# Attention, gated feed-forward and routed experts on one core: the first expert's first matrix in two loads behind the last stores, the late products one accumulator at a time, and a new order of the experts

## Chip, cores and metric

One core of a Trainium2 chip runs the whole program in one launch. The metric is device time in microseconds (us). Engines: PE (TensorE, matrix products), DVE (VectorE), ACT (ScalarE), POOL (GpSimd), SP (SyncE, which here only issues DMAs).

## What is computed

```python
for t in range(S):                                  # attention with a delta-rule state, 32 heads
    y[:, :, t] = einsum('bhd,bhde->bhe', q[:, :, t], state)
    state += beta * k_n (v - state k_n)
...
h = x @ w_in                                        # 3072 x 384 times 384 x 2048
g = P(h) / (Q(h) + 1e-06)                           # P cubic, Q quadratic in |h|
x2 = g @ w_out                                      # 3072 x 384
...
order = argsort(-(x2 @ w_gate).flatten())           # 3072 tokens x 8 experts
# best pairs first; a token goes to one expert, an expert takes at most 384 tokens
for e in range(8):
    out[assigned == e] = relu(x2[assigned == e] @ w1[e]) @ w2[e]
```

The order in which experts fill up depends on the data, so the kernel finds one expert after another: it looks for the first to reach 384 tokens, fixes its tokens, takes expert and tokens out, and looks again.

## The kernel before

The program has a prologue, a loop over 12 chunks of the sequence (attention, feed-forward, gate logits), a drain of the last chunk (`drain`), and the last stage (`tail`) with the choice of experts and their products. All the edits that change the order of work lie between the end of `drain` and the end of the program.

**Late products.** The rows of the last chunk, x2 = g @ w_out, are 96 products of 128x384 into two accumulators in PSUM, px0 and px1 (list `T['late']`, line 1021, 48 products for each). Seven are made in `drain`, the others in `Experts.late` (line 804, products at L761) between the steps of the first choice. ACT moves each accumulator to a tile `yo` (L808), and SP stores it in two DMAs (L809) to the scratch tensor x2d in DRAM, from which the tokens of an expert are gathered.

**The choice of one expert** (`Route.phase`) is a chain between PE and DVE. Six times: count products (L673, or L680 in the first choice), DVE masks the counts (cs, L677), PE folds them (L675), DVE flags full experts (fl, L685), PE spreads the flags (L686), DVE takes the digit (dd, y) and compares anew (ge, L617). `close` then gives the expert's number, the row numbers `ix` of its weights (L706), and the tokens it takes. `perm` turns them into a list of row numbers (pc, o at L739, pD, the list product at L751, `perm` at L757).

**One expert** (`Experts`). `load` (line 778) issues two indirect DMAs from POOL, one for each matrix, 128 rows of 3072 float32 each (L782), and splits each of the 16 pieces of 128x384 into a high part (ACT, L793) and a low part (DVE, L794). `gather` fetches 3 x 128 rows of x2d (POOL, L799). `transp` transposes them on PE (L816) and splits them (xe: ACT L819, DVE L820). `up` has 8 groups of 9 products (L828); after each, ACT takes the relu's high part (L831), and the low part comes from DVE (L833) or, where the table's `rp` is 1 and the planner prefers it, from a product on PE that subtracts the high part (L832) and a relu on ACT (L834). `down` is 3 x 24 products (L841), an eviction to `yo` by ACT (L843) and an indirect store by POOL (L846). Weights are loaded one choice ahead: that of expert k+1 stands between `up` and `down` of expert k.

**What sets the order.** Every step is added to a planner (`Sched`) with an engine, a planned duration, the data that it needs and a priority from the table `PR` (8 numbers for each kind of step, one for each expert). `Sched.run` plays it through and writes out, engine by engine, the order so found; the engines run that order strictly and wait on semaphores, so a step that waits holds up all that stands behind it on its engine. Where the plan shows PE idle before the first transposition, dummy products are put in (L1555).

Of the kernel before, what the change touches and what calls it, by code (L numbers as in the profile page):

```python
# [517 lines left out]
class Ring:  # L518
# [4 lines left out]
PR=dict(cz=[-8460.22,-3349.02,-1040.92,-4662.57,2286.09,-4542.55,-2851.07,-2830.4],  # L523
    hu=[-1158.71,2769.58,-1952.33,1420.35,20.61,-5092.86,1294.98,-2930.25],
    pm=[-827.35,-3434.29,-7199.64,-301.76,-9380.25,-789.5,-2507.28,-3094.98],
    px=[2213.47,-717.87,711.27,1083.3,-50.99,-1678.84,-176.44,-42.49],
    ev=[-2031.38,3896.44,-445.84,4974.79,-456.6,1410.8,-187.26,-280.73],
    rs=[3995.53,-838.36,3724.15,-2030.4,-5106.28,-2002.19,4963.77,-277.67],
    up=[1432.01,7925.78,415.8,19527.06,1302.29,-2496,-1028.3,393.52],
    dn=[-416.52,-263.26,2914.53,2346.47,7002.88,3039.18,1234.23,2541.59],  # L530
    sp=[-1250.53,-1034.63,-3233.17,3355.56,-2061.84,10814.9,2205.04,145.63],
    sq=[1182.66,5658.8,2518.53,1693.88,5502.59,2521.4,11976.42,-493.54],
    ga=[-91.9,220.07,-1393.31,1453.88,1738,-498.56,-1773.97,252.48],
    ld=[-763.16,-1461.53,2155.57,-1535.71,-2478.81,4661.21,334.89,-1356.37],
    sc=[1792.56,3025.86,-3657.49,-269.42,-11268.81,2802.89,972.48,366.12],
    de=[868.62,405.65,-1417.99,2091.14,378.47,2357.24,-3935.23,-63.01],
    rp=[1,0,0,0,0,0,0,0],
    sl=[9.7,-3928.78,-7440.7,1542.96,-6870.28,-1220,4305.31,-2018.78],
    lt=3989.8,
    tol=0.3)  # L540
class Route:
# [3 lines left out]
    def __init__(s,ctx,tc,c):  # L545
# [28 lines left out]
        s.rows=c.tile([128,1],F32,name="rowid"); s.iota(s.rows,[[0,1]],base=128*E,cm=1)  # L574
        s.mk,s.fold={},{}
# [116 lines left out]
    def close(s):  # L692
# [13 lines left out]
        s.V(.07,lambda: v.scalar_tensor_tensor(ix,cm,-128.0,s.rows,op0=OP.mult,op1=OP.add),[cmn],[ixn],.16-z)  # L706
# [55 lines left out]
class Experts:  # L762
# [16 lines left out]
    def load(s,n,ixn,late=[]):  # L779
# [3 lines left out]
        g.add(('POOL',1.038,ld(a,s.w1,"p g j q -> p (g j q)")),[ixd],fa,P1,post=0.7); g.add(('DMA',4.4,None),fa,fa,0,post=0.9)  # L783
        g.add(('POOL',1.038,ld(b,s.w2,"p j f -> p (j f)")),[ixd]+late,fb,P1,post=0.7); g.add(('DMA',4.4,None),fb,fb,0,post=0.9)
# [10 lines left out]
    def gather(s,n,pmn):  # L795
        g=s.g; nc=s.nc; pm,pmd=pmn; s.st.setdefault(n,{})['pm']=pmn; s.st[n]['x']=s.xe.new()
        for i in range(3):
            t,tn=s.xg.new(); s.st[n]['g',i]=t,tn
            g.add(('POOL',1.038,lambda t=t,i=i: nc.gpsimd.indirect_dma_start(out=t,out_offset=None,in_=s.x2d,in_offset=bass.IndirectOffsetOnAxis(ap=pm[:,i:i+1],axis=0))),[pmd,'x2d'],[tn],PR['ga'][n],post=0.7)  # L799
            g.add(('DMA',.55,None),[tn],[tn],0,post=1.0)  # L800
    def late(s,M,T):
# [3 lines left out]
        for bp in range(2):  # L805
# [4 lines left out]
            g.add(('ACT',.371,out),[('epy',bp)],[o_n],20)  # L810
            g.add(('DMA',2.5,None),[o_n],[o_n,'x2d'],0)
# [23 lines left out]
    def down(s,n):  # L835
        g=s.g; nc=s.nc; W2,W2n=s.st[n]['W2']; pm,pmd=s.st[n]['pm']; r,rn=s.st[n]['r']; pd=PR['dn'][n]; pe=PR['de'][n]
        for i in range(3):
# [11 lines left out]
            g.add(('POOL',1.08,out),[o_n,pmd],[('sc',o_n)],PR['sc'][n],post=0.7)  # L849
            g.add(('DMA',.55,None),[('sc',o_n)],[o_n,('sc',o_n)],0,post=1.0)  # L850
LG=1
def tail(R,X,M,T):
    g=R.g=X.g=Sched(); g.tol=PR['tol']; X.late(M,T)
# [126 lines left out]
def drain(g,M,A,R,st,xT,x2d,Lt):  # L980
# [40 lines left out]
    T['late']=[(un,i,bp,gh,wh) for un in range(u0,u0+8) for i in range(2) for bp in range(2) for gh,wh in ((0,0),(0,1),(1,0))]; px=[('px',bp) for bp in range(2)]  # L1021
# [5 lines left out]
    for n,x in enumerate(T['late'][:EL]): add(('PE',.172,go(x,n==0)),[('lg',0),('lg',1)],px if n==0 else [px[x[2]]],1e6+n)  # L1027
# [592 lines left out]
```

## Time and profile before

| | us |
|---|---|
| median of 3 runs (863.96 to 866.63) | 866.54 |
| the profiled execution: time | 867.04 |
| the profiled execution: span, first to last instruction | 865.3 |
| busy over the span: PE, DVE, ACT, POOL | 808.9, 739.5, 563.8, 416.8 |
| mean granted clock of PE, as a share of full speed | 0.979 |

Each row of a timeline has its start and duration in us, counted from the span's first instruction, then engine, line, operation, the names that it writes and reads, and in brackets how long its engine had been idle and what ended that. A row with x9 stands for nine instructions that follow each other. Rows by stretch give for each engine the busy time and the number of instructions, then the granted clock, the busy share of the DMA engines and GB/s. The last late product ends about us 610, the first product of the first expert starts at 626.61, the last product ends about 857.5, and the last stores end the span.

### The profile page before, as it was taken

What the parts mean: (1) busy time and instruction counts of PE and PEld (TensorE: products, weight loads), DVE (VectorE), ACT (ScalarE), POOL (GpSimd) and SP (SyncE); (2) the same over time, 40 slices, a digit from 0 to 9 for tenths busy, and PEclk for the clock granted to TensorE, in tenths of its full rate; (3) what the DMA queues carried; (4) which work ended last, traced back from release to release, by engine and by line L of the source; (5) the groups of instructions that cost most, each with busy time, mean ns of one, the idle gap of its engine ahead of it and who ended that gap; (6) DMA issues with size and microseconds to landing.
All of it is one profiled execution on the core that took longest, in us unless ns stands there. A gap on an engine that the chain in (4) does not pass through costs nothing. (4 is left out here: it accounts for less than half of the span.)

```text
span 865.3 us, 29590 instructions
## 1 busy us (share of the span) xinstructions
PE 808.9 (93%) x12536; PEld 581.0 (67%) x12536; DVE 739.5 (85%) x1696; ACT 563.8 (65%) x1039; POOL 416.8 (48%) x620
## 2 busy tenths in 40 slices
PE   8999789998999999999999999999899899999896
PEld 5887566776677767777777777766556556556563
DVE  8977987888889998998999999996889899889820
ACT  4236767888698787988888889881272451545520
POOL 2256820888678567865786232631221322242501
PEclk9999889999999999999999999999999999999999
DMA  9943387813532524251322201000450542355401
GB/s 362 280 137 84 103 203 211 248 62 75 116 85 81 107 83 97 82 108 31 87 75 67 42 21 39 19 2 20 146 220 29 191 184 112 109 201 229 155 11 45
DMA packets 89588, 98.62 MB, mean 114 GB/s; under 512 B 65776, under 2 KB 73584, under 8 KB 86640
## 3 DMA queue, kind: packets, MB, share of 16 engines
q1 hardware_dynamic: 83072, 59.31, 26.2%
q0 software_dynamic: 6096, 37.23, 11.7%
q8 instruction: 98, 1.61, 0.8%
q14 instruction: 34, 0.28, 0.1%
q10 hardware_dynamic: 288, 0.20, 0.1%
HBM read 74.43 MB, written 17.30 MB: 106 GB/s over the span
## 5 line engine op out<-in xcount | busy, mean ns | idle before, releaser
L936 PEld LDWEIGHTS <-wi 128*128 128x128 f16 x1728 | 168.6, 99 | 38.1 <-issue 6.3
L882 PE MATMUL px<-wo,gg 128*128 128x392 f16 (+1 forms) x1056 | 193.5, 330 | 0.0
L882 PEld LDWEIGHTS <-gg 128*128 128x128 f16 x1056 | 97.8, 98 | 61.8 <-issue 0.7
L900 POOL TENSOR_TENSOR gg<-w,gg 128x512 f16<-128x512 f32 x61 | 71.1, 1166 | 99.6 <-ACT gg L899 92.7
L936 PE MATMUL half<-xT,wi 128*128 128x256 f16 x864 | 107.1, 280 | 3.7 <-DVE wo L1320 2.5
L936 PE MATMUL ph<-xT,wi 128*128 128x256 f16 x864 | 104.2, 275 | 4.5 <-DVE w L913 2.3
L206 POOL TENSOR_TENSOR pmW<-pmW,pmT 128x31 f32<-128x31 f32 (+15 forms) x155 | 89.7, 579 | 10.8
L205 POOL TENSOR_TENSOR pmT<-pmW,pmA 128x31 f32<-128x31 f32 (+15 forms) x155 | 81.3, 525 | 10.9
L841 PEld LDWEIGHTS <-rr 128*128 128x128 f16 x576 | 52.1, 97 | 34.7 <-ACT rr L831 2.8
L846 POOL DMA_INDIRECT out_dram<-yo,perm x24 | 24.3, 1013 | 100.9 <-ACT yo L843 95.5
L831 ACT ACTIVATE rr<-eph 128x384 f16<-128x384 f32 x64 | 30.8, 488 | 59.5 <-PE eph L828 54.4
L899 ACT ACTIVATE gg<-w 128x512 f16<-128x512 f32 x88 | 55.4, 629 | 7.2 <-DVE w L913 6.7
L926 ACT ACTIVATE q<-q 128x512 f32<-128x512 f32 x88 | 54.8, 628 | 4.6 <-DVE q L925 4.5
L841 PE MATMUL px<-wo,rr 128*128 128x384 f16 x288 | 52.7, 330 | 2.4 <-ACT rr L831 2.3
L828 PE MATMUL eph<-xe,w1s 128*128 128x384 f16 x288 | 51.7, 333 | 1.5 <-ACT xe L819 1.0
L841 PE MATMUL px<-w2s,rr 128*128 128x384 f16 x288 | 52.9, 325 | 0.2 <-DVE w2s L794 0.2
L828 PE MATMUL eph<-xe,wo 128*128 128x384 f16 x288 | 51.7, 325 | 0.4 <-ACT xe L819 0.4
L799 POOL DMA_INDIRECT xg<-x2d,perm x24 | 26.4, 1100 | 46.9 <-issue 14.7
L1525 PE MATMUL px<-warm 128*128 128x256 f16 x344 | 44.6, 285 | 2.4 <-DVE warm L1505 2.4
L843 ACT ACTIVATE yo<-px 128x384 f32<-128x384 f32 x24 | 11.5, 490 | 44.9 <-PE px L841 35.7
L828 PEld LDWEIGHTS <-w1s 128*128 128x128 f16 x288 | 26.9, 99 | 19.7 <-issue 3.6
L925 DVE SCALAR_TENSOR_TENSOR q<-q,cf,ph 128x512 f32<-128x512 f32 x44 | 32.4, 737 | 8.7 <-ACT q L919 5.8
(398 smaller groups left out, 1897.6 us busy)
## 6 DMA issues: line engine op xcount, KB each, us to landing
kt<-in_k_dram SPq DMA_DIRECT2D x20, 512.0 KB, 4.5
kn<-in_k_dram SPq DMA_DIRECT2D x12, 384.0 KB, 4.7
qt<-in_q_dram SPq DMA_DIRECT2D x24, 192.0 KB, 3.8
vn<-in_v_dram SPq DMA_DIRECT2D x12, 384.0 KB, 4.4
x2d<-xr SPq DMA_DIRECT2D x44, 96.0 KB, 2.2
xT<-xs SPq DMA_DIRECT2D x22, 144.0 KB, 2.7
wsi<-in_moe_w_in_dram SPq DMA_DIRECT2D x3, 1024.0 KB, 5.4
wst<-in_moe_w_out_dram SPq DMA_DIRECT2D x8, 384.0 KB, 6.2
```

Of the source, the lines that this page charges most:

```text
L205: if half==0: eng.tensor_tensor(t,W[:,0:r,j:j+1].to_broadcast([n,r,k]),A[:,j:j+1,j+1:32].to_broadcast([n,r,k]),op=OP.mult)
L206: else: eng.tensor_tensor(W[:,0:r,j+1:32],W[:,0:r,j+1:32],t,op=OP.subtract)
L828: g.add(('PE',.169,lambda P=P,wh=wh,xh=xh,j=j,f=f,part=part: nc.tensor.matmul(P,W1[:,wh,f,j],xe[:,xh,j],start=(part,j)==(0,0),stop=(part,j ...
L831: g.add(('ACT',.42,lambda P=P,f=f: nc.scalar.activation(r[:,0,f],P,AF.Relu,scale=1.0-2.0**-11)),[Pn],[(rn,0,f)],pe)
L841: g.add(('PE',.17,lambda P=P,rh=rh,wh=wh,f=f,part=part,i=i: nc.tensor.matmul(P,r[:,rh,f,128*i:128*i+128],W2[:,wh,f],start=(f,part)==(0,0), ...
L882: te.matmul(T['px',un//8][bp][:,0:O.N],gg()[:,gh,i,128*bp:128*bp+128],M.wo[:,wh,fb,0:O.N],start=fb==0 and n==0,stop=fb==15 and n==2,skip_g ...
L899: ac.activation(T['gg',un][:,0].rearrange("p f t -> p (f t)")[:,a:b],T['w',un][:,a:b],AF.Copy)
L900: def gl(e): return lambda: e.tensor_tensor(T['gg',un][:,1].rearrange("p f t -> p (f t)")[:,a:b],T['w',un][:,a:b],T['gg',un][:,0].rearrang ...
L925: add(('DVE',.07+.6*z,lambda: ve.scalar_tensor_tensor(q(),q(),cf[:,4:5],P(),op0=OP.add,op1=OP.mult)),Q+Pn,Q,un+O.pd('mu',un))
L926: add(('ACT',.22+.37*z,lambda: ac.activation(q(),q(),AF.Abs)),Q,Q,un+O.pd('f2',un))
L936: for wh,xh in ((0,0),(0,1),(1,0)): te.matmul(T['P',un][:,i],M.wi[:,wh,part,128*fb:128*fb+128],xT()[:,xh,part],start=n==0,stop=n==8); n+=1
L1525: for _ in range(n): nc.tensor.matmul(bk[t or 'px1'][:,0:256],warm[:,0:128],warm,start=True,stop=True)
```

## The change

1. The list of late products has the accumulator as its outermost loop: all 48 products of px0, then all 48 of px1. The two evictions stand where they stood on ACT.
2. The first expert's first matrix comes in two indirect DMAs of 128 rows of 1536. POOL first copies one number from `yo1`, so it waits for the second eviction; then it issues the first half. The second half is issued behind the gathers, right ahead of the second matrix. Row numbers for half rows (`ix2`) are made by one more DVE instruction in the first `close`.
3. Planned durations of the POOL issues become 1.27 us (from 1.038 and 1.08); the planned store of x2d becomes 0.5 us and 2.3 us to landing (from 2.5).
4. The table `PR` is another one, so the order of the last stage is another one. Its `rp` now allows the product L832 for the first three experts (before: for the first).

```diff
-    rp=[1,0,0,0,0,0,0,0],
+    rp=[1,1,1,0,0,0,0,0],
...
+        s.rows2=c.tile([128,2],F32,name="rows2"); s.iota(s.rows2,[[1,2]],base=256*E,cm=2); s.ix2=c.tile([128,2],I32,name="ix2")
...
+        def fx():
+            if first: v.scalar_tensor_tensor(s.ix2,cm.to_broadcast([128,2]),-256.0,s.rows2,op0=OP.mult,op1=OP.add)
+            v.scalar_tensor_tensor(ix,cm,-128.0,s.rows,op0=OP.mult,op1=OP.add)
+        s.V(.07,fx,[cmn],[ixn],.16-z)
...
+        def l1(lo,hi): return lambda: nc.gpsimd.indirect_dma_start(out=a[:,lo:hi].rearrange("p g j q -> p (g j q)"),out_offset=None,in_=s.w1.rearrange('r (h c) -> (r h) c',h=2),in_offset=bass.IndirectOffsetOnAxis(ap=s.ix2[:,lo//4:lo//4+1],axis=0))
+        l2=ld(b,s.w2,"p j f -> p (j f)")
+        def half(): nc.gpsimd.tensor_copy(s.sp,s.yo.t[1][0:1,0:1]); l1(0,4)()
+        def both(): l1(4,8)(); l2()
...
-            g.add(('DMA',2.5,None),[o_n],[o_n,'x2d'],0)
+            k=g.add(('DMA',.5,None),[o_n],[o_n,'x2d'],0,post=2.3)
...
-    T['late']=[(un,i,bp,gh,wh) for un in range(u0,u0+8) for i in range(2) for bp in range(2) for gh,wh in ((0,0),(0,1),(1,0))]; px=[('px',bp) for bp in range(2)]
+    T['late']=[(un,i,bp,gh,wh) for bp in range(2) for un in range(u0,u0+8) for i in range(2) for gh,wh in ((0,0),(0,1),(1,0))]; px=[('px',bp) for bp in range(2)]
```

Over the last stage the new order has 23 products at L832 where there were 8, as many more relus at L834 on ACT, and 41 low parts at L833 on DVE where there were 56. The other counts of the experts' and the choices' steps are the same; two dummy products fewer are made (64 for 66). In the pieces below, the changed program's line numbers are 1 to 11 higher than those of the program before.

POOL at the start of the last stage, before: first the load of the first expert's first matrix, then its gathers.

```order
L782 DMA w1f0_10306<-in_moe2_w1_dram,ix0_10257 128x3072
L799 DMA xg0_10312<-x2d_62,perm0_10281 128x384
L799 DMA xg1_10313<-x2d_62,perm0_10281 128x384
L799 DMA xg2_10314<-x2d_62,perm0_10281 128x384
L782 DMA w2f0_10308<-in_moe2_w2_dram,ix0_10257 128x3072
L782 DMA w1f1_10307<-in_moe2_w1_dram,ix1_10258 128x3072
L782 DMA w2f1_10309<-in_moe2_w2_dram,ix1_10258 128x3072
```

The same place now:

```order
L789 COPY sp_10307<-yo1_10326 1x1
L787 DMA w1f0_10309<-in_moe2_w1_dram,ix2_3670 128x1536
L809 DMA xg0_10315<-x2d_62,perm0_10284 128x384
L809 DMA xg1_10316<-x2d_62,perm0_10284 128x384
L809 DMA xg2_10317<-x2d_62,perm0_10284 128x384
L787 DMA w1f0_10309<-in_moe2_w1_dram,ix2_3670 128x1536
L786 DMA w2f0_10311<-in_moe2_w2_dram,ix0_10260 128x3072
L786 DMA w1f1_10310<-in_moe2_w1_dram,ix1_10261 128x3072
L786 DMA w2f1_10312<-in_moe2_w2_dram,ix1_10261 128x3072
```

A copy that reads `yo1`, and half a matrix, stand ahead of the gathers; the other half has moved behind them.

DVE at the end of the second choice, before, from the expert's number cm1 to its row numbers ix1, from which the second expert's weights are loaded:

```order
L698 TENSOR_REDUCE cm1_10254<-pv1_10252 128x1
L706 SCALAR_TENSOR_TENSOR ix1_10258<-cm1_10254,rowid_3666 128x1
L699 TENSOR_SCALAR pen1_10256<-w8_3657,cm1_10254 128x8
L700 TENSOR_SCALAR ic1_10237<-k21_10223,cm1_10254 128x24
L702 TENSOR_TENSOR Lt_63<-Lt_63,pen1_10256 128x192
```

The same place now, some 20 rows later in the choice, down to ix1:

```order
L706 TENSOR_REDUCE gs1_10248<-go1_10244 128x1
L711 TENSOR_TENSOR lft_10297<-lft_10297,cm1_10257 128x1
L804 SCALAR_TENSOR_TENSOR w1s0_10313<-w1f0_10309,w1s0_10313 128x384
L718 SCALAR_TENSOR_TENSOR ea1_10250<-rp2_10295,eo1_10242 128x24
L709 SCALAR_TENSOR_TENSOR ix1_10261<-cm1_10257,rowid_3666 128x1
```

ix1 stood right behind cm1; now the comparison of the next choice and four low parts of w1s stand between them.

ACT in the relus of the third expert (rr), before, with the high parts of the fourth expert's matrices (from w1f, w2f into wo):

```order
L793 ACTIVATE wo<-w1f_10307 128x384
L831 ACTIVATE rr_10320<-eph_10328 128x384
L793 ACTIVATE wo<-w1f_10307 128x384 x2
L831 ACTIVATE rr_10320<-eph_10325 128x384
L793 ACTIVATE wo<-w1f_10307 128x384 x4
L831 ACTIVATE rr_10320<-eph_10326 128x384
L793 ACTIVATE wo<-w1f_10307 128x384
L793 ACTIVATE wo<-w2f_10309 128x384 x2
L831 ACTIVATE rr_10320<-eph_10327 128x384
L793 ACTIVATE wo<-w2f_10309 128x384 x2
L831 ACTIVATE rr_10320<-eph_10328 128x384
L793 ACTIVATE wo<-w2f_10309 128x384 x3
```

The same place now, to the first eviction:

```order
L842 ACTIVATE rr_10323<-eph_10331 128x384
L845 ACTIVATE rr_10323<-eph_10331 128x384
L842 ACTIVATE rr_10323<-eph_10328 128x384
L854 ACTIVATE yo_10327<-px 128x384
L845 ACTIVATE rr_10323<-eph_10328 128x384
L854 ACTIVATE yo_10325<-px 128x384
L803 ACTIVATE wo<-w1f_10310 128x384 x8
L803 ACTIVATE wo<-w2f_10312 128x384
L854 ACTIVATE yo_10326<-px 128x384
L803 ACTIVATE wo<-w2f_10312 128x384 x7
L830 ACTIVATE xe_10322<-eph_10329 128x3x128
L854 ACTIVATE yo_10327<-px 128x384
```

Before, relus and high parts of the next matrices alternate; now relus come in pairs with the relus behind L832, and the high parts stand behind all of them.

## Rows read from the trace of the kernel before

**Rows 1.** Busy time by stretch of the last stage; the last line is its sum.
```profile
660.00:700.00 40.00, 35.68 (x301) 22.24 (x300) 35.95 (x153) 17.46 (x41) 13.67 (x16) 1.00 0.49 181
...
sum 230.90, PE 216.58 PEld 132.83 DVE 181.19 ACT 103.02 POOL 65.10; mean PE 36.10 PEld 22.14 DVE 30.20 ACT 17.17 POOL 10.85
```

**Rows 2.** Waits of PE, us 626.6 to the end: total, times, longest.
```profile
PE eph L816 <- DMA xg<-x2d,perm: 4.8, 7, 1.4
PE px L841 <- ACT rr L831: 2.3, 1, 2.3
...
PE eph L828 <- ACT xe L819: 1.5, 2, 1.0
```

**Rows 3.** Timeline of the front: start, us, engine, line, operation, [idle before it <- what ended it].
```profile
609.78 0.98 ACT L808 ACTIVATE yo<-px 128x384 f32<-128x384 f32 x2 [19.76 <-PE px L761]
...
610.06 1.10 POOL L782 DMA_INDIRECT w1f<-in_moe_w_dram,ix  x1 [20.22 <-DVE kt L603]
...
610.34 2.37 SPq L809 DMA_DIRECT2D x2d<-yo  x4
...
618.14 0.15 DVE L757 TENSOR_TENSOR perm<-pt,rp 128x3 int32<-128x3 f32 x1
...
618.70 3.42 ACT L793 ACTIVATE w1s<-w1f 128x384 f16<-128x384 f32 x8 [7.93 <-DMA w1f<-in_moe_w_dram,ix]
...
619.77 0.96 POOL L799 DMA_INDIRECT xg<-x2d,perm  x1 [8.61 <-DMA x2d<-yo]
...
626.61 3.00 PE L828 MATMUL eph<-xe,w1s 128*128 128x384 f16 x9
```

**Rows 4.** Issue to landing: stores L809, stores L999, weight loads L782.
```profile
DMA to landing us min/median/max: 6.6/7.0/7.3
DMA to landing us min/median/max: 2.1/2.1/2.1
DMA to landing us min/median/max: 7.1/8.6/11.9
```

**Rows 5.** Busy time by microsecond; the eighth column is the granted clock.
```profile
628.00:629.00 1.00, 1.00 (x5) 0.46 (x3) 0.21 (x1) 0.00 (x0) 0.00 (x0) 0.50 1.02 430
...
740.00:741.00 1.00, 0.40 (x4) 0.18 (x2) 1.00 (x5) 1.00 (x3) 0.70 (x2) 1.00 0.51 160
...
743.00:744.00 1.00, 0.98 (x4) 0.29 (x3) 0.24 (x1) 0.50 (x2) 0.00 (x0) 0.50 0.14 54
```

**Rows 6.** Timeline, second expert's load, its first use, and a wait of PE.
```profile
632.22 1.08 POOL L782 DMA_INDIRECT w1f<-in_moe_w_dram,ix  x1 [7.74 <-DVE ic L700]
...
640.91 1.35 ACT L793 ACTIVATE wo<-w1f 128x384 f16<-128x384 f32 x3 [1.44 <-DMA w1f<-in_moe_w_dram,ix]
...
642.32 0.17 PE L686 MATMUL rp<-fl,ones 128*128 128x8 bf16 x1 [1.24 <-DVE fl L685]
```

**Rows 7.** Timeline, third expert's load, and who stood behind it.
```profile
673.09 1.18 POOL L782 DMA_INDIRECT w1f<-in_moe_w_dram,ix  x1 [0.30 <-DVE y L690]
...
680.38 1.35 ACT L793 ACTIVATE w1s<-w1f 128x384 f16<-128x384 f32 x3 [3.04 <-DMA w1f<-in_moe_w_dram,ix]
...
682.16 0.82 PE L841 MATMUL px<-wo,rr 128*128 128x384 f16 x4 [2.33 <-ACT rr L831]
```

**Rows 8.** From the chain: start, us, what. Fourth load, a split, up products.
```profile
690.96 11.01 DMA w2f<-in_moe_w_dram,ix
...
704.35 0.47 DVE wo L794
...
785.99 6.03 PE eph L828 x37
```

**Rows 9.** Last flag product of a choice: second, third, fourth expert.
```profile
658.18 0.17 PE L686 MATMUL rp<-fl,ones 128*128 128x8 bf16 x1
...
687.15 0.17 PE L686 MATMUL rp<-fl,ones 128*128 128x8 bf16 x1
...
725.50 0.17 PE L686 MATMUL rp<-fl,ones 128*128 128x8 bf16 x1
```

More of the change, by code (lines that the diff above doesn't have):

```diff
@@ L691, in flag, with close @@
             s.V(.88 if DIG[r+1][0]==6 else .5,lambda: s.cmp_(r+1,ge,y2,slice(0,NT)),[y2n],[gn],0)
-    def close(s):
+    def close(s,first=False):
         v=s.nc.vector; te=s.nc.tensor; ra=s.ra; z=s.hurry; bc=[128,E,NT]
@@ L705, in close @@
         s.V(.095,lambda: v.tensor_reduce(gs,go,axis=AX.X,op=OP.add),[gon],[gn],.04)
-        s.V(.07,lambda: v.scalar_tensor_tensor(ix,cm,-128.0,s.rows,op0=OP.mult,op1=OP.add),[cmn],[ixn],.16-z)
+        def fx():
+            if first: v.scalar_tensor_tensor(s.ix2,cm.to_broadcast([128,2]),-256.0,s.rows2,op0=OP.mult,op1=OP.add)
+            v.scalar_tensor_tensor(ix,cm,-128.0,s.rows,op0=OP.mult,op1=OP.add)
+        s.V(.07,fx,[cmn],[ixn],.16-z)
         s.V(.07,lambda: v.tensor_tensor(s.lft,s.lft,cm,op=OP.subtract),[cmn,'lft'],['lft'],.5)
@@ L729, in phase @@
             s.flag(r)
-        return s.close()
+        return s.close(begun)
     def perm(s,nt,p):
@@ L798, in gather @@
             t,tn=s.xg.new(); s.st[n]['g',i]=t,tn
-            g.add(('POOL',1.038,lambda t=t,i=i: nc.gpsimd.indirect_dma_start(out=t,out_offset=None,in_=s.x2d,in_offset=bass.IndirectOffsetOnAxis(ap=pm[:,i:i+1],axis=0))),[pmd,'x2d'],[tn],PR['ga'][n],post=0.7)
+            g.add(('POOL',1.27,lambda t=t,i=i: nc.gpsimd.indirect_dma_start(out=t,out_offset=None,in_=s.x2d,in_offset=bass.IndirectOffsetOnAxis(ap=pm[:,i:i+1],axis=0))),[pmd,'x2d'],[tn],PR['ga'][n],post=0.7)
             g.add(('DMA',.55,None),[tn],[tn],0,post=1.0)
@@ L809, in out @@
                 for half in range(2): r0=(bp+2*half)*S+64*(NCK-1); nc.sync.dma_start(s.x2d[r0:r0+64],o[64*half:64*half+64])
-            g.add(('ACT',.371,out),[('epy',bp)],[o_n],20)
-            g.add(('DMA',2.5,None),[o_n],[o_n,'x2d'],0)
+            g.add(('ACT',.371,out),[('epy',bp)],[o_n,('ev',bp)],20)
+            k=g.add(('DMA',.5,None),[o_n],[o_n,'x2d'],0,post=2.3)
+            if bp: g.t[k][1].pop(k-2,None)
     def transp(s,n,i):
@@ L848, in out @@
                 s.scat.append(d)
-            g.add(('POOL',1.08,out),[o_n,pmd],[('sc',o_n)],PR['sc'][n],post=0.7)
+            g.add(('POOL',1.27,out),[o_n,pmd],[('sc',o_n)],PR['sc'][n],post=0.7)
             g.add(('DMA',.55,None),[('sc',o_n)],[o_n,('sc',o_n)],0,post=1.0)
@@ L852, in tail @@
 def tail(R,X,M,T):
-    g=R.g=X.g=Sched(); g.tol=PR['tol']; X.late(M,T)
+    X.ix2=R.ix2; g=R.g=X.g=Sched(); g.tol=PR['tol']; X.late(M,T)
     R.hurry=PR['hu'][0]; R.cz=PR['cz'][0]; R.pmk=PR['pm'][0]; L={0:R.phase(True)}
@@ L1026, in go @@
         return f
-    for n,x in enumerate(T['late'][:EL]): add(('PE',.172,go(x,n==0)),[('lg',0),('lg',1)],px if n==0 else [px[x[2]]],1e6+n)
+    for n,x in enumerate(T['late'][:EL]): add(('PE',.172,go(x,n==0)),[('lg',0),('lg',1)],px,1e6+n)
     i1=max(i for i in range(len(g.t)) if g.t[i][0][0][0]=='PE')
```

38 lines of the change are left out of this document (20 added, 18 removed).

## The prediction, made before the changed kernel ran

> **What bounds the kernel now.** I read first the busy time by stretch. From the first product of an expert, us 626.6, to the last at 857.5 are 230.9 us; PE is busy in 216.6 of them, DVE in 181.2 [rows 1]. So the last stage is mainly PE's, and what a new order can give is the 14.3 us in which PE stands idle, and what lies ahead of us 626.6. DVE comes close: between us 660 and 700 it is busy 36.0 of 40, PE 35.7 of 40, ACT only 17.5 [rows 1]; a step moved to ACT is free there, one taken off DVE helps whoever waits for DVE.
>
> Next, PE's waits [rows 2]. A third, 4.8 us, is waiting for gathered tokens ahead of the transpositions, seven times; 2.3 us is one wait for a relu; 1.5 us are two waits for the split of transposed tokens. Then the timeline of the front [rows 3]: both evictions of the late rows start at 609.78, when the late products end. The first weight load is issued at 610.06, the four stores from 610.34 on. The token list is ready at 618.29 (618.14 and 0.15), but the gather starts only at 619.77, released by the stores. They took 6.6 to 7.3 us to land, where the same stores one chunk earlier took 2.1 [rows 4]: the load of 1.57 MB was under way at the same time, and its first use is at 618.70 [rows 3]. Last, the clock: in two stretches PE runs at half the granted clock, 1.2 for 2.4 GHz, around us 628 and us 743; the second comes behind a stretch in which PE was busy 0.40 of a microsecond [rows 5].
>
> **The change, part by part.** The sum is made against the profiled execution's 867.04 us, which is 0.5 above the median of 866.54.
>
> *A. Front.* The first accumulator is now complete after 48 products, some ten microseconds earlier, so two of the four stores leave earlier and only those of px1 are left at us 610. The half load is issued behind their eviction and moves half as much. The stores then land within 2.1 to 7.3 us [rows 4] of their issue, which ends at about 611.5: by 613.6 to 618.8, about when the list is ready. The list itself comes 0.1 later for one more small DVE step in the first choice. So the gathers start at about 618.6 instead of 619.8, 1.2 us earlier. Not all of it reaches the first product: three steps of the second choice stand between the transpositions on PE, and they follow DVE's chain. DVE has four splits less in that stretch, worth 0.47 us each [rows 8], but each step still has its round trip over PE. I take half, **-0.6** (bounds -1.2 and 0). Half a load has no row; its bounds are 4.3 us, half of the 8.64 between 610.06 and 618.70 [rows 3], and all 8.6. At either the four pieces needed are there by us 619.5, as they were before. The second half follows the gathers and is needed 37 products after the first, some 9 us later, so I price it at nothing; its cover is the first 36 products, and each microsecond of landing beyond it would cost one.
>
> The Trainium skill, page "DMA: Bandwidth & Descriptors", section "Anatomy of one DMA — SWDGE (gpsimd) path", gives a DMA 2.0 us fixed plus its bytes at 436 GB/s: 3.8 us for half and 5.6 for the whole, so two halves cost 2.0 us more than one whole. It speaks against splitting; the trace's whole load, 8.6 us, is well above it. By that rule, if those 2.0 us lay on the path, A would be +1.4 and the forecast 2.0 later.
>
> *B. Fifteen more products at L832.* 37 products take 6.03 us [rows 8], 0.163 each: **+2.4** on PE. In return DVE loses 15 low parts of 0.47 (7.1 us), and ACT gets 15 relus, which its idle time hides (17.5 busy of 40 [rows 1]); without that they would cost 0.4 or 0.5 each.
>
> *C. Second expert, later.* Its row numbers now come behind the comparison and four splits on DVE, by my count 5 to 6 us later than before. Its load was issued at 632.22, first used at 640.91, and PE waited 1.24 us at 642.32 for a flag behind that use [rows 6]. Now it is issued near 638 and lands, by the same 8.7 us, near 646.5. Eight splits of the first expert's second matrix, 3.8 us, stand between a count and its mask on DVE, while PE has 17 products and two at L832 to fill, 3.1 us. With the round trip I count 0.9 us of wait there, and four more of 0.2 to 0.7 until the second expert's first product: about 3.1 in place of 1.24, so **+1.9** (bounds 0 and +5.1; the upper one with the slowest load, 11.9 us [rows 4]).
>
> *D. Third expert, earlier.* Its load was issued at 673.09, some 14 us after that choice was made (658.18 [rows 9]). ACT then waited 3.04 us for it with two relus behind the high parts, and PE 2.33 us for those relus [rows 7], then 1.0 for a transposed tile [rows 2]. Now its row numbers come right behind the choice, and the load ahead of the gathers. I take both waits off, **-3.4** (bounds -4.3, all that PE idles between 660 and 700 [rows 1], and 0). What may be late next are those gathers, which now queue behind 3.1 MB.
>
> *E. Fourth expert and after.* The fourth load took 11.01 us [rows 8], and ACT had relus of the third expert behind each of its pieces; DVE waited for these relus, and the choice stood still. It took 38.4 us (687.15 to 725.50), the one before it 29.0 (658.18 to 687.15) [rows 9]. Now the third expert's relus stand ahead of those high parts, and their low parts come from PE. A choice that needs 29 us ends some 7 us earlier after the 3.5 us lost in C, and every later gather with it. The longest waits for gathers were the seventh expert's; PE has 65 products between that list and its transpositions, where it had 40, 4.1 us more. So I take off the 4.8 us of waits for gathers [rows 2] and leave all others: **-4.8** (bounds -8.8, the idle time left by C and D in 14.3, and 0).
>
> *F. Clock.* At half clock a product takes twice its 0.163 us. The second stretch, some 3.2 us, cost 1.6; it came behind waits for gathers, so it goes with E: **-1.6** (bounds -3.2, both stretches, and 0).
>
> Sum: -0.6 + 2.4 + 1.9 - 3.4 - 4.8 - 1.6 = -6.1; 867.04 - 6.1 = 860.9, and on the median's scale **860.4 us**. Best ends: -1.2 + 2.4 + 0 - 4.3 - 8.8 - 3.2 = -15.1, 851.4; worst: 0 + 2.4 + 5.1 = +7.5, 874.0. About 0.3%, 2.6 us, is what a measurement can tell from no change.
>
> **Rivals.**
> - *Slower: the second expert's load decides.* Place: POOL has the first expert's first output store ahead of the second expert's gathers, that store waits for an eviction, and the eviction stands on ACT behind seven high parts from this load. By my count the gathers land at 655.2 and are needed at 655.6: 0.4 us of slack. PE has only one product of the first expert left then. From a landing 0.4 us above 8.7 each microsecond costs one; at 11.9 us it is 2.8 more on C, the route stays behind, and neither E nor F comes: -0.6 + 2.4 + 4.7 - 3.4 = +3.1, **869.6**. For it: loads went up to 11.9 [rows 4]. Against: the one it replaces landed in 8.7 with another right behind it, as now.
> - *Same: the waits move.* Strict orders on five engines make new waits where planned and true durations differ; if E and F give nothing and D's gathers wait behind the load for 0.9, the sum is -0.6 + 2.4 + 1.9 - 2.5 = +1.2; with half of E, -1.2: **866.5** between them. For it: DVE is nearly as busy as PE [rows 1].
> - *Better: waits go throughout.* C costs nothing, D and E are whole but for 2 us, F gives both stretches: -0.6 + 2.4 - 11.1 - 3.2 = -12.5; I put this case at **855**, since some of the small waits always stay.
> - *The stores land no earlier*, because they share the DMA engines with whatever half load is there: A is 0, 861.0; part of the forecast.
>
> **How the numbers follow.** Forecast (857.5 to 863.9) 0.60; better 0.13; same 0.16; slower 0.11. Faster by over 0.3%, below 863.9: 0.73; same, to 869.1: 0.17, with a little of the slower case; slower: 0.10. The range 854.5 to 868.0 leaves out most of the slower case and the best end of the better one, 2 in 10. The forecast's own range is 857.5 to 863.9.
>
> **What would show it.** A: the first eviction near us 600 and the first gather near 618.6. C: the second load near 638, and PE's waits between 640 and 660 about 3 us in all. D: third load issued within 2 us of its choice, no wait of 2 us for a relu. E: the fourth choice takes about 29 us, and gathers cost PE under 1 us. F: one stretch at half clock instead of two. Gathers that start at 619.8 again, or waits for gathers of 4 us and more after us 700, would make it wrong.

## The result and the profile after

| | before | after |
|---|---|---|
| median of 14 runs each, us | 863.41 | 856.15 |
| ratio after to before, 95% interval | | 0.9903 (0.9876 to 0.9931) |
| the same pair in a later series, 29 and 12 runs | 867.10 | 860.80, ratio 0.9944 (0.9915 to 0.9972) |
| profiled execution: time, span, mean granted clock | 867.04, 865.3, 0.979 | 856.01, 854.2, 0.986 |
| busy PE, DVE, ACT, POOL | 808.9, 739.5, 563.8, 416.8 | 806.8, 733.0, 570.9, 426.8 |

The kernel became 0.6 to 1.0% faster. The forecast, 860.4 for 866.54, is a ratio of 0.9929, which lies in both intervals. In microseconds the fall is 7.3 and 6.3 for the 6.1 forecast. The time itself, 856.15, lies below the forecast's own range of 857.5 to 863.9, mainly because the kernel before came out at 863.41 in these 14 runs, and the sum had started from 866.54.

The span is 11.1 us shorter, in four parts. The program up to the first choice of an expert, in which the change only puts the late products in another order, ran 1.64 us faster in this execution (its last flag product starts at 605.38, before at 607.02; in the 14 profiles of all kernels it starts between 601.7 and 611.5). From there to the first product of an expert are 19.11 us for 19.59. From the first such product to the end of the last are 221.06 us for 230.32 (before, the last row of products starts at 845.07 and takes 11.86; the 857.5 of the prediction was rounded up). What lies behind is 0.28 longer. So 9.3 of the change's 9.5 us lie between the first and the last product, and there PE idles 5.8 us for 13.75. These are one execution of each kernel: a second one of the changed kernel, `after_again` below, has 20.23 us for the 19.11, 223.66 for the 221.06, and PE idles 8.0.

Busy time by stretch of the changed kernel (PE, PEld, DVE, ACT, POOL, then clock, DMA share, GB/s), for [rows 1]:

```profile
624.49:660.00 35.51, 34.60 (x294) 22.04 (x295) 32.95 (x132) 22.70 (x53) 13.85 (x13) 1.00 0.49 184
660.00:700.00 40.00, 39.65 (x353) 25.15 (x352) 38.72 (x159) 26.26 (x61) 10.47 (x12) 1.00 0.49 185
...
sum 221.06, PE 215.30 PEld 133.79 DVE 176.13 ACT 111.26 POOL 73.81; mean PE 43.06 PEld 26.76 DVE 35.23 ACT 22.25 POOL 14.76
```

Between 660 and 700, where PE idled 4.3 us, it idles 0.35; ACT, which took low parts over from DVE, is busy 26.3 us for 17.5. PE's waits from the first product on, for [rows 2]:

```profile
PE eph L827 <- DVE rr L844: 1.9, 1, 1.9
PE eph L827 <- DMA xg<-x2d,perm: 1.7, 4, 0.7
PE eph L839 <- DVE rr L844: 0.8, 2, 0.5
PE px L852 <- DVE w2s L804: 0.7, 1, 0.7
```

Gathers cost 1.7 us for 4.8; the relu's 2.3 and the 1.5 for the tile of tokens are gone; one wait of 1.9 is new. The timeline of the front, for [rows 3], and the landing of the four stores, for [rows 4]:

```profile
598.74 0.49 ACT L818 ACTIVATE yo<-px 128x384 f32<-128x384 f32 x1 [10.38 <-PE px L765]
...
609.18 0.18 POOL L789 COPY sp<-yo 1x1 f32<-1x1 f32 x1 [20.99 <-ACT yo L818]
610.03 2.26 POOL L787 DMA_INDIRECT w1f<-in_moe_w_dram,ix  x1 [0.68 <-DVE pcs L744]
616.41 1.76 ACT L803 ACTIVATE w1s<-w1f 128x384 f16<-128x384 f32 x4 [7.30 <-DMA w1f<-in_moe_w_dram,ix]
616.98 1.08 POOL L809 DMA_INDIRECT xg<-x2d,perm  x1 [4.68 <-DVE perm L761]
...
x2d<-yo SPq DMA_DIRECT2D x4, 96.0 KB, 2.1
```

The stores land in 2.1 us for 7.0 (medians of the landings that the traces hold), and the gather is released by the token list (`perm`), no longer by the stores. The second and the third expert's loads and their first uses, and the last flag products of the choices, for [rows 6, 7, 9]:

```profile
634.29 0.96 POOL L786 DMA_INDIRECT w1f<-in_moe_w_dram,ix  x1 [10.70 <-DVE di L665]
635.55 4.50 POOL L786 DMA_INDIRECT w2f<-in_moe_w_dram,ix  x1 [0.30 <-issue]
...
641.25 2.99 ACT L803 ACTIVATE wo<-w1f 128x384 f16<-128x384 f32 x7
...
657.86 1.12 POOL L786 DMA_INDIRECT w1f<-in_moe_w_dram,ix  x1 [2.01 <-DVE ic L701]
...
665.36 1.35 ACT L803 ACTIVATE w1s<-w1f 128x384 f16<-128x384 f32 x3 [0.42 <-DMA w1f<-in_moe_w_dram,ix]
```

```profile
656.54 0.17 PE L687 MATMUL rp<-fl,ones 128*128 128x8 bf16 x1
...
684.02 0.17 PE L687 MATMUL rp<-fl,ones 128*128 128x8 bf16 x1
...
708.35 0.17 PE L687 MATMUL rp<-fl,ones 128*128 128x8 bf16 x1
```

The third load leaves 1.3 us behind its choice and costs ACT 0.42 us for 3.04. The fourth choice takes 24.3 us for 38.4.

### The profile page after: what moved, and what is told of

Its sections match the earlier page's. It is cut to its first block, busy times and chain, and to the rows that moved or that the text cites. A ratio compares the mean times of both kernels' runs of the same rounds, so it can differ in the third digit from the quotient of the medians.

```text
span 854.2 us, 29621 instructions
## 1 busy us (share of the span) xinstructions
PE 806.8 (94%) x12549; PEld 581.2 (68%) x12549; DVE 733.0 (86%) x1682; ACT 570.9 (67%) x1054; POOL 426.8 (50%) x623
## 4 chain that ended last, share of the span: by engine, by line
PE 50%; DVE 19%; issue 10%; DMA 8%; POOL 7%; ACT 3%; SPq 2%; POOLq 0%; ACTq 0%
PE px L893 12%; PE half L947 8%; PE ph L947 7%; PE eph L839 4%; PE px L852 3%; DMA xg<-x2d,perm 3%; POOL pmW L206 2%; PE px L1536 2%; POOL pmT L205 2%; PE tg L123 2%; PE tg L269 2%; PE px L765 1%; DMA w2f<-in_moe_w_dram,ix 1%; DVE w L924 1%; PE tg L260 1%
## 5 line engine op out<-in xcount | busy, mean ns | idle before, releaser
L206 POOL TENSOR_TENSOR pmW<-pmW,pmT 128x31 f32<-128x31 f32 (+15 forms) x155 | 87.7, 566 | 10.8
L857 POOL DMA_INDIRECT out_dram<-yo,perm x24 | 26.5, 1105 | 79.2 <-ACT yo L854 69.3
L839 PE MATMUL eph<-xe,w1s 128*128 128x384 f16 x288 | 55.1, 332 | 0.9 <-DVE rr L844 0.8
L839 PE MATMUL eph<-xe,wo 128*128 128x384 f16 x288 | 49.3, 325 | 0.0
L809 POOL DMA_INDIRECT xg<-x2d,perm x24 | 27.9, 1161 | 32.7 <-PE eph L839 12.1
L1536 PEld LDWEIGHTS <-warm 128*128 128x128 f16 x352 | 33.8, 101 | 9.3 <-DVE warm L1516 2.4
```

What stands on the lines that cost most here:

```text
L206: else: eng.tensor_tensor(W[:,0:r,j+1:32],W[:,0:r,j+1:32],t,op=OP.subtract)
L839: g.add(('PE',.169,lambda P=P,wh=wh,xh=xh,j=j,f=f,part=part: nc.tensor.matmul(P,W1[:,wh,f,j],xe[:,xh,j],start=(part,j)==(0,0),stop=(part,j ...
L1536: for _ in range(n): nc.tensor.matmul(bk[t or 'px1'][:,0:256],warm[:,0:128],warm,start=True,stop=True)
```

## The experiments

In all but two the planner's order was kept, and only what a step emits was changed, so that every other instruction stands on its engine where it stood. `w2late14` and its twin are planned anew, from one late place on. Each table has, from the profile of each kernel, the time from the first choice's last flag product to the first product of an expert ("front"), from there to the end of the last product ("experts"), and the stretches at half the granted clock (1.2 for 2.4 GHz) of 3 us and more between the first choice and the last product; one costs about 1.6 us where PE is busy. Beside each median stands that of the kernel before in the same series, so only rows with the same one can be compared by their medians; front and experts are of one execution each.

**1. Front and order apart.** `order_alone`: the changed kernel, in whose `load` and list

```diff
-        def half(): nc.gpsimd.tensor_copy(s.sp,s.yo.t[1][0:1,0:1]); l1(0,4)()
-        def both(): l1(4,8)(); l2()
+        def half(): ld(a,s.w1,"p g j q -> p (g j q)")()
+        def both(): l2()
...
-    T['late']=[(un,i,bp,gh,wh) for bp in range(2) for un in range(u0,u0+8) for i in range(2) for gh,wh in ((0,0),(0,1),(1,0))]
+    T['late']=[(un,i,bp,gh,wh) for un in range(u0,u0+8) for i in range(2) for bp in range(2) for gh,wh in ((0,0),(0,1),(1,0))]
```

> The changed program with its front put back and every other instruction in the changed order: the late products alternate between the accumulators again, the first matrix comes whole, and POOL does not wait for the second eviction. Theory 1 (the new order of the experts carries the gain, terms C, D and E): -6 to -8 us against the kernel before, ratio 0.991 to 0.993, PE's waits after the first product near 6 us, the first gather near 619.8 on the scale of the profile before. Rival (the front carries it, by earlier tokens and by the half-clock stretch that goes with them): -1 to -3 us, ratio 0.9965 to 0.999. Whether the half-clock stretch at the first expert's start comes back is open: if it does, it costs 1.6 us more.

`front_alone`: the kernel before with the new list, the copy and the half load behind the second eviction, and the second half behind the gathers (`def both()` and `def half()` as in the change, called at those places).

> The kernel before with the new front and its own order otherwise: late products one accumulator at a time, POOL waits for the second eviction and loads half of the first matrix, the second half follows the gathers. Theory 1: -0.5 to -1.2 us from earlier gathers, and -1.6 if the half-clock stretch at the first expert's start goes with them, ratio 0.997 to 0.9995; the third load, the wait of 3 us on ACT and the 38 us of the fourth choice stay as they were. Rival: -4 us and more, ratio below 0.9955.

`front_whole`: the same, but `half` loads all of the matrix, and there is no second half.

> The kernel before with the new front but one whole load of the first matrix behind the second eviction, not two halves. Theory (in the old order the second half is what cost: DVE stands at its pieces with the second choice queued behind them): no wait of 6 us for a flag, the time within 2 us of the kernel before, ratio 0.998 to 1.002. Rival (waiting for the eviction, or the list, costs as well): ratio 1.003 to 1.008.

`whole_copy`: the changed kernel with `half` loading the whole matrix behind the copy. `oldlist`: the changed kernel with the old list alone.

> The changed program with the first matrix in one whole load at the place of the first half, still behind the second eviction; no second half. Theory 1: the half gains nothing but the stores' landing. If the 1.57 MB in flight delay the stores as in the kernel before, the gathers start about 1 us later and the high parts of the first matrix a further 1 to 2 us later, and the time is 0.5 to 2 us above the changed kernel (ratio 0.991 to 0.993). If the stores, already issued first, are not delayed, it is within 0.5 us of the changed kernel. Rival (two loads cost 2 us more than one): 1 to 2 us below the changed kernel, ratio 0.988 to 0.9895.

> The changed program with the late products in the old list, alternating between the two accumulators, all else as changed. Both evictions then stand at the end of the products, as before; all four stores leave together. Theory 1: the first gather 0.3 to 1.2 us later than in the changed kernel, the time 0 to 1 us above it (ratio 0.9903 to 0.9915). Rival (the list does nothing, since the last two stores set the gathers either way): no difference in the first gather above 0.2 us.

| | median, before | ratio (95%) | front | experts | at half clock |
|---|---|---|---|---|---|
| before | | | 19.59 | 230.32 | 2 |
| after | 856.15, 863.41 | 0.9903 (0.9876 to 0.9931) | 19.11 | 221.06 | 1 |
| order_alone | 853.63, 862.35 | 0.9913 (0.9888 to 0.9939) | 19.10 | 218.65 | 0 |
| oldlist | 853.84, 862.35 | 0.9916 (0.9885 to 0.9948) | 19.16 | 218.27 | 0 |
| whole_copy | 857.28, 862.35 | 0.9933 (0.9910 to 0.9956) | 20.45 | 220.19 | 1 |
| front_alone | 868.50, 862.35 | 1.0081 (1.0054 to 1.0109) | 25.75 | 225.30 | 2 |
| front_whole | 864.46, 864.14 | 1.0000 (0.9971 to 1.0029) | 21.55 | 225.82 | 1 |

The order alone gives the whole gain, and its front is as short as the changed kernel's, although the load is whole and nothing waits for the eviction. But not all of its stores land quickly (the last line is theirs):

```profile
607.47 2.37 SPq L819 DMA_DIRECT2D x2d<-yo  x4
607.81 1.10 POOL L786 DMA_INDIRECT w1f<-in_moe_w_dram,ix  x1 [20.84 <-DVE q L609]
...
616.34 0.96 POOL L809 DMA_INDIRECT xg<-x2d,perm  x1 [7.43 <-DVE ge L618]
...
DMA to landing us min/median/max: 2.0/2.2/6.7
```

The first store leaves 0.34 us ahead of the load here; in the kernel before it left 0.28 behind [rows 3]. The first two stores, 0.34 us ahead of the load and 0.2 behind it, land in 2.0 and 2.2 us; the third, 0.8 us behind it, takes 6.7 (the trace has no landing of the fourth), and the first gather stands 12.2 us behind the first choice, for 11.6 in the changed kernel. The first product does not come later for it. The list alone moves nothing: with the old list the first gather still stands 11.6 us behind the first choice. The half load brings the first high parts 2.1 us sooner (11.0 us behind the first choice, 13.1 in `whole_copy`) and the first product up to 1.3, which the runs cannot tell apart: the four kernels that have the front of before in the old order (before, `third_early`, `low_pe`, `low_pe_third`) have fronts from 19.6 to 20.9 us. `whole_copy` ends just above the range of its first theory. In the old order the new front makes the kernel 0.8% slower, against both expectations. The profile of `front_alone` shows where, in rows of ACT, DVE and PE:

```profile
622.80 1.76 ACT L804 ACTIVATE w1s<-w1f 128x384 f16<-128x384 f32 x4 [8.18 <-DMA w1f<-in_moe_w_dram,ix]
...
623.36 0.56 DVE L805 SCALAR_TENSOR_TENSOR w1s<-w1f,w1s 128x384 f16<-128x384 f32 x1 [6.58 <-ACT w1s L804]
623.83 0.16 DVE L686 TENSOR_SCALAR fl<-rp 128x8 bf16<-128x8 f32 x1
...
624.04 0.17 PE L687 MATMUL rp<-fl,ones 128*128 128x8 bf16 x1 [6.85 <-DVE fl L686]
```

In that order the fifth piece's split stands on DVE ahead of a flag of the second choice. The second half comes late, DVE waits 6.6 us for the piece, and PE 6.85 for the flag that was ready to be made. In the new order this split stands behind that choice. With the whole load (`front_whole`) this wait is gone (one of 2.0 us for a masked count, cs, stands there), and the medians show no loss. The execution profiled of `front_alone` took 862.93, the fastest of its six, since its program up to the first choice was 5.3 us faster than that of before. From the first choice to the last product it took 251.1 us for 249.9: its experts took 5 us less, its front 6.2 more. So this profile shows about 1 of the 6 us that the median lost, and where the rest lies was not settled.

**2. The third load and the products on PE, each alone.** `third_early`: the kernel before; the third expert's row numbers are made right behind its choice and its loads issued there.

```diff
+            v.tensor_reduce(cm,x,axis=AX.X,op=OP.max)
+            if ph==2: v.scalar_tensor_tensor(ix,cm,-128.0,s.rows,op0=OP.mult,op1=OP.add); s.hook[2]()
...
+        if n==2: e1,e2=l1,l2; s.R.hook[2]=lambda: (e1(),e2()); l1=l2=lambda: None
```

> The kernel before with one thing moved: the third expert's row numbers are made right behind its choice on DVE, and its two loads are issued then, ahead of the second expert's last outputs or right behind them, near us 659.5 instead of 673.09. Theory 1 (D as priced: the late load alone makes the waits of 3.04 us on ACT and 2.33 us on PE): those two waits go, and the time falls by 2.3 to 4.3 us, ratio 0.995 to 0.9975; the fourth choice still takes over 36 us. Rival (a wait taken out of a fixed order comes back at the next late input): PE's waits between 660 and 700 fall by 2 us and more, but later waits grow, and the time stays within 1 us, ratio 0.999 to 1.001.

`low_pe`: the kernel before; where DVE made a low part of the second or third expert, now

```diff
+            def lowp(P=P,f=f): nc.tensor.matmul(P,s.neg,r[:,0,f],start=False,stop=True,skip_group_check=True); nc.scalar.activation(r[:,1,f],P,AF.Relu)
```

> The kernel before with the 16 low parts of the second and third expert made by a product on PE and a relu on ACT, at the place where DVE made them; every other instruction stands in the order of before. Theory 1 (the products relieve DVE, which paces the choice, in any order): DVE loses 8 us of work, PE gains 2.6, the time falls by 3 to 6 us, ratio 0.993 to 0.9965. Rival (the gain needs the new order, in which these relus stand ahead of the next weights on ACT; in the old one the third expert's relus stand behind each piece of a load): within 2 us of the kernel before, ratio 0.998 to 1.002, or slower by the 2.6 us on PE.

`low_pe_third`: both of these.

> Both single edits in the old order: the third expert's loads right behind its choice, and the 16 low parts on PE and ACT. Theory 1: the two add up or do better together, since the choice of the fourth expert is now held by neither, -5 to -8 us, ratio 0.991 to 0.994, the fourth choice below 34 us. Rival (only an order found anew turns them into time): no more than the better one of them alone, ratio above 0.996.

`rp_undo`: the changed kernel with the products of the second and third expert taken out; DVE makes these 15 low parts, `scalar_tensor_tensor(r[:,1,f],P,0.0,r[:,0,f],op0=OP.max,op1=OP.subtract)`, at the product's place in the order.

> The changed program with the 15 low parts that moved to PE and ACT (second and third expert) back on DVE, at the place of the product; every other instruction stands in the changed order. Theory 1 (these products pay for themselves, because DVE paces the choice where it is busy 19 of 20 us): PE loses 2.4 us of work, DVE gets 8 us, PE's waits for DVE between 650 and 700 grow by 4 us and more, and the time is 2 to 5 us above the changed kernel, ratio 0.992 to 0.996. Rival (B as priced, with cover on DVE): 1 to 2.4 us below it, ratio 0.9875 to 0.989.

`after_again` is the changed kernel beside `rp_undo`, for the comparison and for the clock.

> The changed kernel itself once more, beside the others. Ratio 0.988 to 0.993. Open: whether the stretch at half clock behind the wait of 1.93 us near us 805 comes again. If the wait makes it, it comes; if it is a matter of when the clock is judged, it may stay away, as in three of the four variants that have the same wait, and the part from the first product to the last is then about 219 us instead of 221.

| | median, before | ratio (95%) | front | experts | at half clock |
|---|---|---|---|---|---|
| third_early | 864.42, 867.10 | 0.9977 (0.9954 to 0.9999) | 20.88 | 228.50 | 1 |
| low_pe | 870.32, 864.14 | 1.0058 (1.0028 to 1.0088) | 20.73 | 234.73 | 1 |
| low_pe_third | 865.62, 864.14 | 0.9998 (0.9970 to 1.0026) | 20.36 | 231.62 | 2 |
| rp_undo | 865.79, 867.10 | 0.9993 (0.9966 to 1.0019) | 20.34 | 231.22 | 2 |
| after_again | 860.80, 867.10 | 0.9944 (0.9915 to 0.9972) | 20.23 | 223.66 | 1 |

No part of the new order does in the old one what it does here. The early load takes its two waits away, but the experts are only 1.8 us shorter, and one stretch at half clock less makes 1.6 of that. Busy time in equal stretches, counted from the first product of an expert, first of `third_early`, then of the kernel before: the third choice, the fourth, and the stretch behind the last.

```profile
657.18:686.18 29.00, 26.34 (x228) 16.42 (x226) 26.83 (x110) 11.74 (x28) 7.84 (x9) 1.00 0.39 144
686.18:724.18 38.00, 36.62 (x296) 22.85 (x294) 36.08 (x124) 16.87 (x40) 10.05 (x13) 1.00 0.33 115
...
782.18:854.18 72.00, 68.52 (x431) 41.25 (x429) 39.02 (x106) 29.58 (x67) 20.07 (x27) 1.00 0.34 126
```

```profile
658.11:687.11 29.00, 24.68 (x218) 15.59 (x217) 25.57 (x102) 10.02 (x23) 6.42 (x8) 1.00 0.39 144
687.11:725.11 38.00, 37.07 (x295) 22.94 (x294) 36.06 (x122) 18.02 (x43) 8.60 (x11) 1.00 0.31 115
...
783.11:855.11 72.00, 69.11 (x436) 41.62 (x434) 40.99 (x117) 30.48 (x69) 20.73 (x27) 1.00 0.34 124
```

PE's idle time falls from 4.32 to 2.66 us in the first and grows from 0.93 to 1.38 in the second and from 2.89 to 3.48 in the last; over all seven stretches it is 13.8 for 13.75. In the trace the rival is right; by the times the kernel became 0.0 to 0.5% faster, which lies between the two expectations, so a small gain is likely and its place is not shown. Both edits together, `low_pe_third`, give nothing.

The products alone make the old order slower. Fourth choice, `low_pe` and its ACT:

```profile
690.22:730.75 40.53, 38.67 (x306) 23.78 (x305) 32.68 (x116) 21.69 (x52) 9.14 (x11) 1.00 0.30 108
```

```profile
701.19 0.49 ACT L832 ACTIVATE rr<-eph 128x384 f16<-128x384 f32 x1
701.57 0.51 ACT L793 ACTIVATE wo<-w1f 128x384 f16<-128x384 f32 x1
701.99 0.48 ACT L831 ACTIVATE rr<-eph 128x384 f16<-128x384 f32 x1
```

DVE is now idle for 7.9 us of this choice, and the choice takes 40.5 us for 38.4. So it was not DVE's load alone that held it. The relus stand one by one between the pieces of the fourth load on ACT, each new one with its half microsecond, and DVE now waits 6.4 us for ACT's split of the tokens (before 1.1 us, in the same two choices):

```profile
DVE xe L820 <- ACT xe L819: 6.4, 2, 5.3
```

That ACT is what holds the choice is argued from these rows and was not tested by itself. In the changed order the products pay. `rp_undo` and `after_again`, third choice:

```profile
667.79:699.25 31.46, 26.55 (x226) 15.60 (x224) 31.04 (x115) 14.11 (x32) 4.94 (x5) 1.00 0.34 125
```

```profile
658.85:686.97 28.12, 27.12 (x239) 17.12 (x237) 26.17 (x103) 19.12 (x44) 5.00 (x5) 1.00 0.37 139
```

Without the products DVE is busy in all but 0.42 us, PE idles 4.9 us for 1.0, and the experts take 7.6 us more (1.6 of it one more stretch at half clock); by the medians the kernel loses 5.0 of the 6.3 us that the change had won on this chip, more than expected (`after_again` itself came out at 0.9944 for the 0.988 to 0.993 expected). The execution profiled of `rp_undo` is its slowest, 873.57 us, but 7.6 us of that lie ahead of the first choice, outside these stretches. The fourth choice of `rp_undo`, with DVE's low parts and the third expert's relus ahead of the weights, stays short, 26.4 us for 24.9 in `after_again` and 38.4 before; its two ends:

```profile
699.25 0.17 PE L687 MATMUL rp<-fl,ones 128*128 128x8 bf16 x1 [0.26 <-DVE fl L686]
...
725.64 0.17 PE L687 MATMUL rp<-fl,ones 128*128 128x8 bf16 x1
```

So the new order shortens this choice, and the products do not.

**3. A planned landing.** `w2late14` and, with the front of `order_alone`, `oa_w2late14`:

```diff
-        g.add(('DMA',4.4,None),fb+([] if n else [('h',0)]),fb,0,post=0.9)
+        g.add(('DMA',14 if n==7 else 4.4,None),fb+([] if n else [('h',0)]),fb,0,post=0.9)
```

> The changed kernel with one planned duration more: the landing of the last expert's second matrix is planned at 14 us instead of 4.4, so that its splits stand behind the seventh expert's relus on ACT and DVE; the order before that place is the same. Theory (ACT waits 3.44 us for this matrix with the relus behind it, and PE then 0.53, 0.25 and 1.93 us for their low parts): these waits go, the last product comes 2 to 2.7 us sooner, ratio 0.986 to 0.9885 if no other wait takes their place. Rival (the splits become late for the last expert's own products): a wait for the split of the second matrix in the last 25 us, no gain.

> The changed order with the last expert's second matrix planned to land late, and with the old front (old late list, the first matrix whole, no wait for the eviction). Theory (the front is worth nothing in this order, the planned landing 2 to 3 us): ratio 0.986 to 0.990, the last stage as long as with the new front within 1 us once stretches at half clock are taken off. Rival (the new front is worth about 1 us here): ratio above 0.990.

| | median, before | ratio (95%) | front | experts | at half clock |
|---|---|---|---|---|---|
| w2late14 | 857.55, 867.10 | 0.9898 (0.9860 to 0.9936) | 20.00 | 220.52 | 1 |
| oa_w2late14 | 855.56, 864.14 | 0.9867 (0.9829 to 0.9906) | 19.67 | 219.04 | 1 |

In the changed kernel ACT waits for the last expert's second matrix with the seventh expert's relus behind its pieces:

```profile
796.65 1.35 ACT L803 ACTIVATE wo<-w2f 128x384 f16<-128x384 f32 x3 [3.44 <-DMA w2f<-in_moe_w_dram,ix]
797.91 0.47 ACT L842 ACTIVATE rr<-eph 128x384 f16<-128x384 f32 x1
```

PE then waits 2.7 us for their low parts (0.53, 0.25 and 1.93). Planned late, the pieces stand behind the relus. PE's timeline there, and its stretch behind the last choice, in `w2late14`:

```profile
799.35 10.89 PE L839 MATMUL eph<-xe,w1s 128*128 128x384 f16 x66
...
776.80:847.34 70.54, 70.45 (x448) 43.18 (x446) 39.49 (x113) 30.71 (x69) 26.41 (x27) 1.00 0.35 132
```

The 66 products run through, and behind the last choice PE idles 0.1 us, where `after_again` idles 2.8 in 73.94. Both kernels beat the one before. Against the changed kernel on the same chip, `w2late14` is 3.3 us faster by the medians and 3.1 in the experts of the trace; the intervals of the two ratios overlap (0.9936 and 0.9915), the runs themselves hardly (854.34 to 859.92 and 858.07 to 867.17). Its ratio is a little above the 0.986 to 0.9885 expected. The old front does not hurt here either.

## Why the prediction was right, step by step

By the times the sum came true, its terms only in part. Here is each term in the two executions of the changed kernel, against the one of the kernel before, up to the last product. C, D and E are PE's idle time up to us 660, to 700 and behind; a stretch at half clock counts 1.6 us, and B is what is left of PE's busy time.

| | forecast | after | after_again |
|---|---|---|---|
| A, front | -0.6 | -0.5 | +0.6 |
| B, products | +2.4 | +0.3 | +0.7 |
| C, second load | +1.9 | -0.8 | 0.0 |
| D, third load | -3.4 | -4.0 | -3.3 |
| E, fourth choice and later | -4.8 | -3.2 | -2.4 |
| F, clock | -1.6 | -1.6 | -1.6 |
| sum | -6.1 | -9.7 | -6.0 |

B and C cost about 2 us less each than forecast, and E gave 1.6 to 2.4 less. These errors offset each other, so that the sum fits is in part luck.

**A, front.** The mechanism came as forecast, the size by luck. The stores land quickly and the first gather starts 1.15 us earlier, counted from the first choice; of that 0.48 us reach the first product in one execution, and in `after_again`, with the same gather, the front is longer than before. The load in flight did hold up the stores, as I had read it: in `order_alone` the third store, issued 0.8 us behind the start of the whole load, takes 6.7 us. What frees them is the wait for the eviction, which holds the load back until the last stores go out; `oldlist` and `whole_copy`, which keep that wait, have quick stores with the old list and with the whole load. But no run shows that an earlier gather is worth anything: `order_alone` has neither list nor half load nor wait, its gather stands 0.6 us later, and its front is 19.10 us long. That the second half's "cover is the first 36 products" is not enough in the old order; `front_alone` shows what it costs there.

The Trainium skill, page "DMA: Bandwidth & Descriptors", section "Anatomy of one DMA — SWDGE (gpsimd) path", would have a half land in 3.8 us and the whole in 5.6. Here all three took longer: the first half was in use 6.4 us behind the start of its issue, the second landed in 5.2, and the whole load of `whole_copy` in 8.3. That two halves cost more than one whole, 2.0 us by the page's figures, the trace bears out with 3.3, but not on the path: `whole_copy`, with the whole load at the place of the half, has a front of 20.45 us and so none shorter.

**B, products: +2.4 forecast, +0.3 and +0.7 measured.** PE's busy time went from 216.57 to 215.30 with one stretch of 1.6 at half clock less. `rp_undo` against `after_again` gives about 1 for the same 15 products, once their one and two stretches are taken off. A product that follows a wait shows its whole 0.33 us in the rows, one in a row 0.163; fewer waits would explain the rest, which is argued and not tested.

**C, second load: +1.9 forecast, 0 to -0.8 measured.** The load left at 634.29, not near 638, since the second choice took 21.8 us for 23.9, and was in use 7.0 us later, with no wait. PE idles 0.9 us up to us 660, before 1.75; in `after_again` 1.74. I had counted DVE's steps rightly as later (the load leaves 7.1 us behind its choice, before 1.3), but counted their round trips as waits of PE, which had products to fill them: between 640 and 660 I expected about 3 us of waits, and PE idles 0.1. With B this is the largest error of the sum.

**D, third load: -3.4 forecast, -4.0 and -3.3 measured** between 660 and 700. Its mechanism stands in the rows (0.42 us of wait for 3.04). As a term of a sum it fell: `third_early` shows that the same move alone gives 0 in the trace and at most 0.5% by the times.

**E, fourth choice and later gathers: -4.8 forecast, -3.2 and -2.4 measured** (idle time behind us 700: 4.50 and 5.25 for 7.68). The choice took 24.3 us, less than my 29, and gathers 1.7 us for the under 1 that I named. What ate the rest is the wait of 1.9 us at 805.10, which I had not seen and which `w2late14` removes. That relus between the pieces of the load made the fourth choice long fits `low_pe` and `rp_undo`; no run moved these relus alone. The long choice by itself cost little: PE idled 0.9 of its 38 us.

**F, clock: -1.6 forecast and measured, by accident.** I forecast the stretch at the start to stay and the one at 743 to go. In the changed kernel both were gone, and a new one came behind the wait at 805.10. In `after_again`, the same program, the start runs at half clock, and there is none behind the same wait. First `after_again`, then the changed kernel, each with its first product behind the wait and PE's busy time and granted clock in a microsecond shortly after:

```profile
809.04 0.61 PE L827 MATMUL eph<-ident,xg 128*128 128x128 f32 x3 [1.93 <-DVE rr L844]
...
811.00:812.00 1.00, 1.00 (x8) 1.00 0.00 0
```

```profile
805.10 0.61 PE L827 MATMUL eph<-ident,xg 128*128 128x128 f32 x3 [1.93 <-DVE rr L844]
...
807.00:808.00 1.00, 1.00 (x5) 0.50 0.00 0
```

Which waits are followed by such a stretch belongs to an execution, not to the order alone. The Trainium skill, page "TensorE: Matmul & The Clock Gate", section "Part 1: The HAM clock gate (the "warmup" mystery)", says that the window in which the chip watches PE runs freely and is not reset by a kernel, with which these two executions agree; no run shows the window itself.

**The rivals.** The second load did not decide. The better case came half true: C cost nothing and D was whole, E was not, and one stretch of two went; 856.15 lies nearer to its 855 than to 860.4. The rival in which waits move did not happen to the change as a whole, but it is what the trace of `third_early` shows for the early load tried alone. The stores did land earlier.

## What to carry to other kernels

Where engines run strict orders, a new order is one thing: take its parts singly into the old order and they give little (0.0 to 0.5%) or cost something (0.6%), take the products on PE out of the new order and most of the gain goes; so bound such a change by the idle time of the engine that limits the stage (13.8 us here, of which 8.0 and 5.8 came in two executions), and do not trust a sum over moved steps term by term. Before a step is moved to an engine that seems free, read what stands beside it in that engine's order: ACT was idle more than half the time, and still relus put between the pieces of a load made the kernel 0.6% slower. In a planner, the duration of a late transfer is worth as much as its priorities: one number, 14 for 4.4, gave about 3 us.

## What the runs showed of the hardware

- Stores of 96 KB issued ahead of a load of 1.57 MB or up to 0.3 us behind the start of its issue landed in 2.0 to 2.2 us; those issued 0.8 us behind it and later took 6.3 to 7.6 us (the kernel before, `order_alone`, `third_early`, `low_pe`, `low_pe_third`, `oa_w2late14`; some landings are not in the traces).
- The issue of an indirect load, gather or store on POOL took at most 1.4 us in 59 of 65 cases behind us 600 of the changed kernel, but 4.50 us at 635.55, 4.62 at 785.60 and, for a gather, 3.09 at 791.84; `after_again` has 4.50, 4.61 and 3.09 at the same steps. Each of these fell beside an unbroken row of weight splits on DVE (635.40 to 639.24, 785.57 to 789.41, 790.71 to 794.08), as did those of 3 us and more in the other profiles read for this. Shorter issues met single splits, and no run tested the cause.
- The same program, with the same wait of 1.93 us of PE, is followed by three microseconds at half clock in one execution and by none in another.
- The part of the program up to the first choice, in which no edit does more than reorder the late products, ended between 601.7 and 611.5 us in the 14 profiles, and the 14 runs of the kernel before spread from 860.14 to 872.09; medians of a few runs cannot tell 0.3% here.
